# Counting the first pass of a TensorE run as longer, in the planner of a fused attention and feed-forward kernel

## The chip, the cores and the metric

The kernel runs on one core of a Trainium2 chip. The metric is the device time of one launch in microseconds, the median of a few runs of the same program. Times of single instructions come from one profiled execution, whose own time stands beside the runs below.

## The reference

The input x has 2048 rows of 640 values. It is normalised row by row, and two branches and the input itself are added up:

```python
xn = _layernorm(x, axis=-1)
return x + _A_ref(xn, A_wq, A_wk, A_wv, A_wo) + _B_ref(xn, B_w1, B_w2)

# A: 32 query heads of 20 values, one key head and one value head shared by all
q = (xn @ wq).reshape(B, S, 32, 20).transpose(0, 2, 1, 3)
k, v = xn @ wk, xn @ wv
p = softmax(einsum("bhqd,bkd->bhqk", q, k) * 20 ** -0.5)
A = einsum("bhqk,bkd->bhqd", p, v).reshape(B, S, 640) @ wo

# B: feed-forward, 640 -> 1728 -> 640
B = silu(xn @ w1) @ w2
```

The costly part is attention: 32 heads times 2048 queries times 2048 keys, that is 134 million exponentials.

## The kernel before, in words

**Tiling.** Queries are cut into 4 blocks of 512 columns, heads into 8 groups of 4, which gives 32 groups of work. Within a group the keys are cut into 16 tiles of 128. One item of work is the score tile of one head: 128 keys by 512 queries. There are 32 x 16 x 4 = 2048 items. A head has only 20 values, so its score product uses 32 of the TensorE array's 128 rows: four heads lie in four row tiles and run side by side when their instructions follow one another (line 1078, `s_mm`). In the text such a bundle is a set of scores.

**Two ways to the exponential.** Most items go to ScalarE (ACT in the profile): one ACTIVATE takes two or three score banks at once and writes exponentials (line 1166). The others go in batches of four (one key tile, four heads) to VectorE (DVE), which adds a constant to the score and writes a 16-bit integer whose bits, read as bf16, are roughly the exponential (line 1409, `p1`). Two more copies of the batch, shifted by a constant, correct that approximation; they are made by GpSimd (POOL, line 1448) or by VectorE (line 1453).

**Passes.** What is left on TensorE uses the array as four column tiles of 32 columns: the product of exponentials and values (line 1201, one pass for a key tile on ScalarE's way, three for a batch on VectorE's way, because of its shifted copies), and the projections, the feed-forward and the output product (line 447, passes of 512 columns, or of 320 for the output). A pass is four MATMULs, one for each column tile. Some output passes can be cut into row pieces that ride in a set of scores (line 454, `row_mm`). In the text a sequence of passes between two sets of scores is a run.

**Who sets the order.** The program has a fixed instruction order on each engine. A planner in Python (class `Sched`, the function `build`) makes it before the launch: it keeps a clock for each engine, gives each operation a cost in nanoseconds, and at each step commits the operation that the engine with the earliest clock would take. Engines then wait for each other on the chip by semaphores in that order. So a cost in the planner is no time on the chip; it changes only which operation is picked next. The clock of TensorE is advanced in `Sched.commit` by an operation's cost, and by `SWITCH` (97 ns to a set of scores, 98 ns to a run) when the array's use changes. `t_mc` is the cost of a pass of projections, feed-forward or output; the passes on the exponentials have a cost written at the two places that make them (`make_pv_act`, `dve_advance`). A set of n scores counts 216 + 4(n - 1) ns.

**The rule string.** The choices have thresholds (`BASE`): how far ahead of ScalarE a set of scores is issued (`need`, `hold`, `stay`), how many batches may be open at once (`open`), how long a set waits for a third bank (`patience`), whether output passes are cut into row pieces (`rows`, `half`). The string `PLAN` gives one letter to each stretch of the planner's TensorE clock, and `RULES` says which threshold the letter alters; behind the end of the string the letter is "a", which alters nothing. `PIECE` is the length of a stretch:

```python
if sc.t["pe"] >= piece * PIECE:
    ru.__dict__.update(BASE)
    ru.__dict__.update(RULES[rule(piece)])
    piece += 1
```

The letters that the prediction names: B and G cut passes of the output into row pieces (`rows` 2 or 1), f waits up to 200 ns for a third bank, J puts sets of scores off while ScalarE has more than 560 ns of work ahead, r lets VectorE's items in from 1000 ns ahead, t allows three open batches, x allows a second pass job to be begun while four banks are free, z sends every shifted copy but the third to VectorE.

Of the kernel before, what the change touches and what calls it, by code (L numbers as in the profile page):

```python
# [53 lines left out]
WAY_S = {"act": 55.0, "dve": 57.0, "pool": 57.0}  # L54
WAY_B = 57.0
SLACK_B = 1.0
WAY_DMA = -130.0
ACT_END = 104.0
DVE_END = 85.0
# [22 lines left out]
POOL_J = (2,)  # L82
SWITCH = {"s": 97.0, "p": 98.0, "f": 98.0}
SPRIO = 0.5
PIECE = 10000.0
STEPS = 1
YC = (0, 0, 3, 3)
EARLY = 1
# [17 lines left out]
RULES = dict(a={}, b=dict(keep=0.0), c=dict(lagp=3), d=dict(lagp=5), e=dict(lagp=0), f=dict(patience=200.0), g=dict(dwant=0.0),  # L106
             h=dict(zcap=4), i=dict(zcap=3), j=dict(homes=0), k=dict(leadmax=-1.0, lead=-1.0), l=dict(lead=0.08, leadmax=0.1),
             m=dict(need=740.0), n=dict(hold=0.0), o=dict(stay=640.0), p=dict(open=1), q=dict(slack=560.0), r=dict(hungry=1000.0), s=dict(claim=9), t=dict(open=3), u=dict(claim=4), v=dict(want=2), w=dict(slack=850.0), x=dict(hold2=4), y=dict(bnd=0), z=dict(pj=-1e9), A=dict(rows=0), B=dict(rows=2, rowmin=2), C=dict(pj=2000.0), D=dict(openlag=3), E=dict(pj=8000.0), F=dict(hold2=3), G=dict(rows=1), H=dict(half=0), I=dict(half=3), J=dict(stay=560.0), K=dict(stay=720.0), P=dict(need=560.0), Q=dict(hold=120.0), L=dict(uopen=3), M=dict(uopen=4), N=dict(uopen=5), O=dict(uopen=0))
PLAN = "acbgxnoQpQJvpnaQodtxzpvEoQJBJoaodpJqQaDqJovpkBrnvxBxQJBfaaooHoatano"


def rule(n):
# [55 lines left out]


def t_mc(n):  # L170
    return n / 2.4 + (9.0 if n >= 512 else 4.0)


def t_mm(n):
# [37 lines left out]
class Sched:  # L212
# [33 lines left out]
    def way(self, h, op):  # L246
        if h.eng == op.eng:
            return 0.0
        if h.dma_sem is not None:
            return WAY_DMA  # L250
        if op.eng == "pe":
# [33 lines left out]
    def commit(self, op, start):  # L285
        e = op.eng
        op.deps = self.hazards(op)
        if op.sync is not None:
            op.deps.add(op.sync)
        op.start = start  # L290
        if e == "pe":
            if op.mode != self.pe_mode:
                start += self.turn(op.mode)
                self.pe_mode = op.mode
            s0 = self.joined(op)
            if s0 is not None:
                end = max(start + op.occ, self.pe_set[2])
                self.pe_set = (s0, self.pe_set[1] | op.slots, end)
                op.fin = start + op.occ + 170.0
                op.occ = end - self.t[e]  # L300
                self.t[e] = end
            else:
                op.fin = start + op.occ + 170.0
                self.t[e] = start + op.occ
                self.pe_set = (start, op.slots, start + op.occ) if op.slots else None
        elif e == "sp":
            self.t[e] = start + op.occ
            own = 3300.0 if op.name == "dma wv" else 800.0 if op.name.startswith("dma pk") else 2000.0 if op.name.startswith("dma la") else 0.0
            self.dma_free = max(self.dma_free, start + 1300.0) + (op.lat - 800.0 if op.name.startswith("dma pk") else op.lat)
            op.fin = self.dma_free + 700.0 + own  # L310
        else:
            if op.port and e == "dve" and start > self.t[e] and start <= self.port_free["pool"] + 1.0:
                op.occ -= PORT_HID
            op.fin = start + op.occ + op.lat
            self.t[e] = start + op.occ
            if op.port:
                self.port_free[e] = start + op.occ - (PORT_GAP if e == "pool" else 0.0)
        op.done = True
        for r in op.reads:
            r.r.append(op)  # L320
        for r in op.writes:
            r.w = op
            r.r = []
        self.order[e].append(op)
        if op.on_commit is not None:
            op.on_commit(op)


def build(nc, A_x, A_wq, A_wk, A_wv, A_wo, B_x, B_w1, B_w2, out, stack):
# [90 lines left out]
    def res(*k):  # L420
        if k not in R:
            R[k] = Res()
        return R[k]
# [58 lines left out]
    def load_x(n):  # L482
# [9 lines left out]
         reads=[res("idf")], writes=[res("idf")], prio=0.02)  # L492
# [10 lines left out]
    def zeros(n, k=QW):  # L503
# [5 lines left out]
              reads=[res("zero")], writes=[res("v")], prio=0.6)  # L509
    v1s = []  # L510
    for j, cj in enumerate(C_J):
        v1s.append(pool(lambda g, j=j, cj=cj: g.memset(v_all[:, j, :, DH:DH + 1], 0.5 * cj), 120,
                        pre=[vms], writes=[res("v")], prio=0.6 + 0.01 * j))

    def wrow(ap):
# [6 lines left out]
                  reads=[res("wk")], writes=[res("wkr", r)], prio=0.08) for r in range(1, HG)]  # L522
# [4 lines left out]
    for n in range(8, NT):  # L527
# [11 lines left out]
        reads=[res("wqs0")], pre=[pool_wq0, d_wq0], writes=[res("wqp0")], prio=0.15)  # L539
# [97 lines left out]
    v_op = {}  # L637
# [568 lines left out]
    def make_pv_act(g, kt, d):  # L1206
        flags = {}

        def f(pe):
            lst = []  # L1210
            for i in range(HG):
                k = d[i][0]
                lst.append((v_all[:, 0, kt, :], Ebuf[:, k * QW:(k + 1) * QW], i))
            return pv_mms(pe, flags["bank"], lst, flags["first"], flags["last"])
        op = Op("pe", f, 224.0, pre=[x[1] for x in d.values()] + v_op[kt // 4],
                reads=[res("E", x[0]) for x in d.values()] + [res("vv", kt // 4, 0)],
                mode="p", prio=1.0, name=f"PV{g}_{kt}")
        pv_reg(op, g, flags)
        return op
# [200 lines left out]
    def dve_advance(job):  # L1420
        st = job.batch
        st["left"].remove(job.head)
        st["p1"].append(job.consumers[0])
        if st["left"]:
            return
        open_b.remove(st)
        g, kt, zi = st["g"], st["kt"], st["zi"]
        z = z_t[zi]
        zr = [res("z", zi, i) for i in range(HG)]
        N = HG * QW  # L1430
        closed.append(st)
        z16 = z[:, :].bitcast(I16)
        st["nth"] = len(closed)
        src = [([z[:, i * QW:(i + 1) * QW] for i in range(HG)], st["p1"], zr)]
        for j in range(1, NJ):
            qk = XQ[j - 1]
            if qk is not None and len(s_last[j - 1]) == NW[j - 1] and len(xq_read[qk]) == DC + FC and all(o.done for o in xq_read[qk]):
                s_last[j - 1].append(sc.order["pe"][-1])
            wi = min(range(len(s_last[j - 1])), key=lambda k: -1 if s_last[j - 1][k] is None or k == NW[j - 1] and isinstance(s_last[j - 1][k], Op) else s_last[j - 1][k]["nth"])
            old = s_last[j - 1][wi]  # L1440
            s_last[j - 1][wi] = st
            lent = wi == NW[j - 1]
            t = xnT[:, 0:HG, qk * QW:(qk + 1) * QW] if lent else s_t[j - 1][wi][:, :]
            zin = z16.rearrange("p (h q) -> p h q", h=HG) if lent else z16
            r = res("s", j, wi)
            args = dict(pre=st["p1"] + ([idb] + [norm_op[n] for n in range(NT)] if old is None else [old] if isinstance(old, Op) else [old["pv"][j]]), reads=zr, writes=[r], name=f"s{j}")
            if j in POOL_J or pool_load() < ru.pj:
                op = pool(lambda v, t=t, j=j, zin=zin: v.tensor_scalar(t.bitcast(I16), zin, float(SHIFT[j]), 1.0, ALU.add, ALU.mult),  # L1448
                          POOL_SHIFT, POOL_END, prio=0.3, **args)
                op.port = True  # L1450
                op.gate = calm(op)
            else:
                op = dve(lambda v, t=t, j=j, zin=zin: v.tensor_scalar_add(t.bitcast(I16), zin, float(SHIFT[j])), t_dve(N, 4),  # L1453
                         prio=SPRIO - 0.01 * j, **args)
                op.port = True
                op.on_commit = shifts.append
            src.append(([t[:, i, :] if lent else t[:, i * QW:(i + 1) * QW] for i in range(HG)], [op], [r]))
        st["sh"] = [pre[0] for _, pre, _ in src[1:]]
        st["pv"] = []
        for j, (t, pre, rd) in enumerate(src):  # L1460
            flags = {}

            def f(pe, t=t, j=j, flags=flags):
                lst = [(v_all[:, j, kt, :], t[i], i) for i in range(HG)]
                return pv_mms(pe, flags["bank"], lst, flags["first"], flags["last"])
            pv = Op("pe", f, 224.0, pre=pre + v_op[kt // 4], reads=rd + [res("vv", kt // 4, j)],
                    mode="p", prio=1.5, name=f"PVd{g}_{kt}")
            pv_reg(pv, g, flags)
            st["pv"].append(pv)
# [71 lines left out]
    def make_two():  # L1541
# [8 lines left out]
                   pre=[norm_op[n] for n in range(NT)] + [o for n in range(NT) for o in tr_ops[n]] if k else [])  # L1550
# [88 lines left out]
    def take(job, e):  # L1639
        b = job.fixed  # L1640
        if b is None:
            ok = [b for b in xbanks() if bank_at(b, job.ops[0].mode) <= e + SLACK_B]
            b = (min(ok, key=lambda b: (-left_over(sc.free, (b,)), HOME_ORDER.index(b))) if ru.homes else max(ok)) if ok else min(xbanks(), key=bank_free_at)
# [340 lines left out]
    while not finished():  # L1984
        if sc.t["pe"] >= piece * PIECE:
            ru.__dict__.update(BASE)
# [13 lines left out]
        es, op, what = got  # L2000
# [173 lines left out]
```

## Time and profile before

| what | value |
|---|---|
| time, median of 3 runs | 689.98 us (689.96 to 690.01) |
| the profiled execution's own time | 690.16 us |
| its span, first to last instruction | 688.3 us |
| granted TensorE clock | 1.00 |
| TensorE busy | 675.7 us (98%) |
| ScalarE busy | 666.4 us (97%) |
| VectorE busy | 591.3 us (86%) |
| GpSimd busy | 581.7 us (85%) |
| ACTIVATEs of exponentials | 656 |
| items on VectorE's way | 676, that is 169 batches |

The profile names engines PE (TensorE), PEld (its weight loads), ACT, DVE, POOL and SP (the queue of DMAs). A group's row gives the line of the kernel, the engine, the operation, the tiles written and read, their size, the count, the busy time and the mean. The row of a window gives its bounds, its length, and for each engine the busy time and the count of instructions in it. A row of the timeline gives the start and the length of a stretch of like instructions. Records of neighbouring instructions on an engine overlap, so the distance between two starts says what an instruction costs its engine, and the record's own length says more than that.

### The profile page before, as it was taken

The page shows a single profiled execution, that of the slowest core. Times are in us where ns is not written, and L with a number is a line of the kernel's source. Part 1 is how long each engine was busy: PE and PEld are TensorE (multiplying, and loading weights), DVE is VectorE, ACT ScalarE, POOL GpSimd, SP SyncE. Part 2 cuts the span into 40 slices and gives each one's busy share as a digit, 9 for nine tenths or more (in the row PEclk, how much of TensorE's full clock was granted, in tenths as well). Part 3 has the DMA queues.
Part 4 walks back from the last instruction along what each step waited for, and adds up shares of the span by engine and source line. Part 5 has one row for each costly group of instructions (what it writes and reads, how often), then busy time and mean ns, then how long its engine had stood idle before and what let it go on. Part 6 is the DMA issues. An engine that isn't in the chain of part 4 may idle for free.

```text
span 688.3 us, 22511 instructions
## 1 busy us (share of the span) xinstructions
PE 675.7 (98%) x9821; PEld 232.2 (34%) x9821; DVE 591.3 (86%) x1017; ACT 666.4 (97%) x728; POOL 581.7 (85%) x349
## 2 busy tenths in 40 slices
PE   8999999999999999999999999999999999999998
PEld 6432222222333333322323333332233333333345
DVE  7899988999989878798898897889999898987953
ACT  6999999999999999999999999999999999999992
POOL 6658899898988998899898889888889987879990
PEclk9999999999999999999999999999999999999999
DMA  8643220222221222422022222132222221223201
GB/s 226 190 160 42 19 23 14 35 34 25 23 29 12 32 38 29 72 36 30 9 22 30 29 31 33 26 37 61 31 22 20 21 27 23 32 20 70 23 7 41
DMA packets 34241, 28.97 MB, mean 42 GB/s; under 512 B 15486, under 2 KB 29662, under 8 KB 34142
## 3 DMA queue, kind: packets, MB, share of 16 engines
q1 hardware_dynamic: 33854, 27.20, 25.8%
q8 instruction: 77, 1.26, 0.8%
q10 hardware_dynamic: 288, 0.33, 0.1%
q14 instruction: 22, 0.18, 0.1%
HBM read 11.09 MB, written 2.62 MB: 20 GB/s over the span
## 4 chain that ended last, share of the span: by engine, by line
ACT 52%; PE 42%; DVE 3%; POOL 1%; DMA 0%; issue 0%; DVEq 0%; ACTq 0%
ACT sbt L1166 48%; PE psall L1201 14%; PE psall L1078 14%; PE psall L447 13%; ACT sbt L773 3%; DVE sbt L1409 2%; POOL sbt L1448 1%; PE psall L595 1%; PE psall L621 1%; DVE sbt L1453 0%; DMA sbt<-in_A_x_dram 0%; PE psall L999 0%; PE psall L1017 0%; ACT sbt L554 0%; DVE sbt L565 0%
## 5 line engine op out<-in xcount | busy, mean ns | idle before, releaser
L1166 ACT ACTIVATE sbt<-psall 128x1024 bf16<-128x1024 f32 (+1 forms) x656 | 640.0, 1138 | 3.2 <-PE psall L1078 3.0
L1448 POOL TENSOR_SCALAR sbt<-sbt 128x2048 int16<-128x2048 int16 x273 | 518.6, 1900 | 72.5 <-PE psall L1201 15.3
L1409 DVE TENSOR_SCALAR sbt<-psall 128x512 int16<-128x512 f32 x676 | 440.1, 685 | 63.1 <-PE psall L1078 58.0
L1078 PE MATMUL psall<-sbt 32*128 32x512 bf16 x2048 | 268.3, 384 | 3.3 <-ACT sbt L1166 2.0
L1201 PE MATMUL psall<-sbt 128*32 128x512 bf16 x3400 | 264.7, 384 | 1.9 <-POOL sbt L1448 0.6
L447 PE MATMUL psall<-sbt 128*32 128x320 bf16 (+2 forms) x3772 | 225.9, 332 | 2.1 <-DVE sbt L776 0.7
L1078 PEld LDWEIGHTS psall<-sbt 32*128 32x128 bf16 x2048 | 71.8, 91 | 236.9 <-ACT sbt L1166 174.1
L447 PEld LDWEIGHTS psall<-sbt 128*32 128x32 bf16 x3772 | 80.4, 95 | 85.5 <-issue 45.4
L1201 PEld LDWEIGHTS psall<-sbt 128*32 128x32 bf16 x3400 | 68.8, 94 | 115.5 <-issue 71.9
L1453 DVE TENSOR_SCALAR sbt<-sbt 128x2048 int16<-128x2048 int16 x65 | 47.6, 750 | 0.0
L860 POOL TENSOR_TENSOR sbt<-sbt 128x512 bf16<-128x512 f32 x30 | 38.3, 1277 | 4.9 <-DVE sbt L1453 2.7
L776 DVE SCALAR_TENSOR_TENSOR sbt<-sbt,psall 128x512 bf16<-128x512 bf16 x52 | 35.5, 682 | 3.8 <-ACT sbt L773 1.8
L773 ACT ACTIVATE sbt<-psall 128x512 bf16<-128x512 f32 x52 | 34.9, 671 | 0.2 <-PE psall L447 0.2
L454 PE MATMUL psall<-sbt 32*128 32x320 bf16 (+1 forms) x78 | 24.4, 313 | 0.0
L1250 DVE COPY sbt<-psall 128x512 f32<-128x512 f32 x31 | 21.2, 683 | 0.9 <-PE psall L1201 0.8
L919 DVE SCALAR_TENSOR_TENSOR sbt<-psall,sbt 128x320 f32<-128x320 f32 x8 | 3.9, 491 | 12.2 <-PE psall L447 7.0
L903 DVE SCALAR_TENSOR_TENSOR sbt<-psall,sbt 128x320 bf16<-128x320 f32 x24 | 11.6, 482 | 3.1 <-PE psall L447 1.7
L693 DVE TENSOR_SCALAR sbt<-psall 128x512 bf16<-128x512 f32 x20 | 13.5, 676 | 0.0
L572 POOL TENSOR_TENSOR sbt<-sbt 128x2 f32<-128x2 f32 x8 | 5.7, 710 | 8.5 <-DVE sbt L570 8.2
L1725 PE MATMUL psall<-sbt 128*32 128x256 bf16 (+1 forms) x188 | 11.1, 375 | 1.2 <-DVE sbt L487 1.2
L585 POOL TENSOR_SCALAR sbt<-sbt 128x640 bf16<-128x640 bf16 x12 | 10.4, 878 | 1.5 <-DVE sbt L577 1.5
L563 DVE BATCH_NORM_STATS2 sbt<-sbt 128x6 f32<-128x320 bf16 x14 | 6.6, 472 | 2.0 <-DMA sbt<-in_A_x_dram 2.0
(64 smaller groups left out, 118.3 us busy)
## 6 DMA issues: line engine op xcount, KB each, us to landing
sbt<-sbt SPq DMA_DIRECT2D x120, 64.0 KB, 3.8
sbt<-in_A_x_dram SPq DMA_DIRECT2D x28, 160.0 KB, 3.9
sbt<-sbt SPq DMA_DIRECT2D x213, 20.0 KB
out_dram<-sbt SPq DMA_DIRECT2D x14, 160.0 KB, 2.2
sbt<-in_B_w_dram SPq DMA_DIRECT2D x1, 2160.0 KB, 11.5
sbt<-in_B_w_dram SPq DMA_DIRECT2D x1, 2080.0 KB, 8.2
sbt<-sbt SPq DMA_DIRECT2D x75, 8.0 KB
sbt<-in_A_wq_dram SPq DMA_DIRECT2D x1, 800.0 KB, 6.7
```

Source lines behind the costliest of these rows:

```text
L447: ins = pe.matmul(ps[j * SLOT:(j + 1) * SLOT, b * BANK + off:b * BANK + off + n], w[:, j * SLOT:(j + 1) * SLOT], x, start=start, stop=stop ...
L454: return pe.matmul(ps[0:w.shape[-1], b * BANK:b * BANK + n], w[k], x[k], start=start, stop=stop, tile_position=(r * SLOT, 0))
L773: t = Op("act", lambda a: a.activation(t_buf[0:rows, ts, :], bk(job.bank, 0, QW, rows=rows), AF.Tanh, scale=0.5), t_act(512), ACT_END, pre ...
L776: u = Op("dve", lambda v: v.scalar_tensor_tensor(out=hT[par][0:rows, fk, :], in0=t_buf[0:rows, ts, :], scalar=1.0, in1=bk(job.bank, 0, QW, ...
L860: nm = pool(lambda e: e.tensor_tensor(oU[:, us, :], U_sb[:, us, :], Rrep, ALU.mult), 1356.0, POOL_END, pre=[uc] + lc + pack_op.get(divmod( ...
L1078: return pe.matmul(bk(b), kT_rep[i * SLOT:(i + 1) * SLOT, kt * P:(kt + 1) * P], qT[i * SLOT:(i + 1) * SLOT, g % NQ, :], start=True, stop=T ...
L1166: return a.activation(Ebuf[:, es * QW:es * QW + w], ps[:, buf[0] * BANK:buf[0] * BANK + w], AF.Exp, scale=ESCALE)
L1201: ins = pe.matmul(ps[i * SLOT:(i + 1) * SLOT, ub * BANK:ub * BANK + QW], lhsT, rhs, start=(first and k < HG), stop=(last and k >= len(lst) ...
L1250: return v.tensor_copy(U_sb[:, us, :], bk(ub))
L1409: p1 = Op("dve", lambda v: v.tensor_scalar(z16[:, i * QW:(i + 1) * QW], bk(job.bank), ZBIAS, 0.0, ALU.add, ALU.max), t_dve(QW) + 2.0, DVE_ ...
L1448: op = pool(lambda v, t=t, j=j, zin=zin: v.tensor_scalar(t.bitcast(I16), zin, float(SHIFT[j]), 1.0, ALU.add, ALU.mult), POOL_SHIFT, POOL_E ...
L1453: op = dve(lambda v, t=t, j=j, zin=zin: v.tensor_scalar_add(t.bitcast(I16), zin, float(SHIFT[j])), t_dve(N, 4), prio=SPRIO - 0.01 * j, **args)
```

## The change

Three things are altered in the planner, and no instruction of its own is added.

1. The cost of a pass on the exponentials falls from 224 to 216 ns, that of other passes by 6.3 ns (512 columns and more) or 1.3 ns (fewer). 10.4 ns are added to the first pass behind a change from another use of the array.
2. A stretch of the rule string lasts 16 us of the planner's clock instead of 10.
3. The string is another one, of 42 letters instead of 67.

```diff
+FIRST = 10.4
+PASS = 216.0
...
-PIECE = 10000.0
+PIECE = 16000.0
...
-PLAN = "acbgxnoQpQJvpnaQodtxzpvEoQJBJoaodpJqQaDqJovpkBrnvxBxQJBfaaooHoatano"
+PLAN = "apQxxcJBxtrJJfBfKcrJhoGzBKGvErjzBrPBBaaJto"
...
 def t_mc(n):
-    return n / 2.4 + (9.0 if n >= 512 else 4.0)
+    return n / 2.4 + 2.7
...
         if e == "pe":
             if op.mode != self.pe_mode:
                 start += self.turn(op.mode)
+                if op.mode == "p":
+                    op.occ += FIRST
                 self.pe_mode = op.mode
...
-        op = Op("pe", f, 224.0, pre=[x[1] for x in d.values()] + v_op[kt // 4],
+        op = Op("pe", f, PASS, pre=[x[1] for x in d.values()] + v_op[kt // 4],
...
-            pv = Op("pe", f, 224.0, pre=pre + v_op[kt // 4], reads=rd + [res("vv", kt // 4, j)],
+            pv = Op("pe", f, PASS, pre=pre + v_op[kt // 4], reads=rd + [res("vv", kt // 4, j)],
```

## The prediction

> **What bounds the kernel now.** I read the first and the fourth part of the page, then ScalarE's groups by shape, then windows of 100 us.
>
> ```profile
> span 688.3 us, 22511 instructions
> PE 675.7 (98%) x9821; PEld 232.2 (34%) x9821; DVE 591.3 (86%) x1017; ACT 666.4 (97%) x728; POOL 581.7 (85%) x349
> ACT 52%; PE 42%; DVE 3%; POOL 1%; DMA 0%; issue 0%; DVEq 0%; ACTq 0%
> ```
>
> Two engines are full, and the chain that ended last alternates between them. Busy shares don't say which one gives way, so the cost of one instruction is read from distances between starts, on ScalarE first.
>
> ```profile
> L1166 ACT ACTIVATE sbt<-psall 128x1024 bf16<-128x1024 f32 x594 | 563.5, 1100 | 2.6 <-PE psall L1078 2.5
> L1166 ACT ACTIVATE sbt<-psall 128x1536 bf16<-128x1536 f32 x61 | 89.7, 1512 | 0.6 <-PE psall L1078 0.6
> 299.68 4.76 ACT L1166 ACTIVATE sbt<-psall 128x1024 bf16<-128x1024 f32 x5
> 304.20 0.73 ACT L773 ACTIVATE sbt<-psall 128x512 bf16<-128x512 f32 x1
> 304.68 3.92 ACT L1166 ACTIVATE sbt<-psall 128x1024 bf16<-128x1024 f32 x4
> ACT sbt L1166 <- PE psall L1078: 3.0, 7, 0.6
> sum 500.00, ACT 485.06; mean ACT 97.01
> ```
>
> Five exponentials of two banks take 304.20 - 299.68 = 4.52 us, 0.904 us each, and the tanh behind them 0.48 us. The waits of ScalarE for scores come to 3.0 us in 7 places. The sum is that of five windows of 100 us from 100 to 600 us, for line 1166 alone: 97.01 of 100 us, and the tanh fills most of the rest. In steady state ScalarE has no room.
>
> TensorE comes next, as a stretch of its timeline (rows between are left out).
>
> ```profile
> 301.02 0.39 PE L1078 MATMUL psall<-sbt 32*128 32x512 bf16 x3
> 301.34 0.62 PE L447 MATMUL psall<-sbt 128*32 128x512 bf16 x8
> 301.89 0.39 PE L1078 MATMUL psall<-sbt 32*128 32x512 bf16 x3
> ...
> 304.82 0.83 PE L1201 MATMUL psall<-sbt 128*32 128x512 bf16 x12
> 305.48 0.60 PE L447 MATMUL psall<-sbt 128*32 128x512 bf16 x8
> ...
> 311.90 0.39 PE L1078 MATMUL psall<-sbt 32*128 32x512 bf16 x3
> ```
>
> A set of scores is followed 0.32 us later by a run (301.34 - 301.02). Three passes take 0.66 us (305.48 - 304.82), 0.22 each. A run of two passes reaches the next set after 0.55 us (301.89 - 301.34), which is 0.11 us more than two passes. So a set with the turn to it and back costs 0.32 + 0.11 = 0.43 us, and a pass 0.22 us.
>
> **The change part by part: the costs.** A cost moves nothing on the chip by itself; every instruction of an unchanged order would run as before. What it can do is make the planner's clock right or wrong. From 301.02 to 311.90 us there are 11 cycles of set and run, with 28 passes of 512 columns. The kernel before counts 11 x (224 + 98 + 97) + 28 x 224 = 10,881 ns; the trace has 10.88 us. The kernel after counts 11 x (224 + 98 + 97 + 10.4) + 28 x 216 = 10,771 ns, which is 0.11 us short, 10 ns for each run. The reason is in the rows: the first pass is now counted as longer, but the last one loses the 8 ns that stood for the rest of its turn. The old costs are right for a run of two to three passes and too high for long ones; the new ones are about equally short for all runs, so they rank long against short runs better, and stand worse against ScalarE's clock, whose costs are unchanged. With 656 ACTIVATEs, and about one set for each, the clock of TensorE is short by up to 656 x 10 = 6.6 us. Price on the chip: 0, where sets of scores are issued early enough that 10 ns are lost in their lead; up to +6.6 us, where each set comes late for ScalarE by that much; a gain of as much is excluded, for the order can take nothing from an instruction. I take 0, because ScalarE waited only 7 times, which is the nearest row. It holds as long as the lead holds; without that cover ScalarE waits next, for line 1078.
>
> **The change part by part: the string.** What a string can move is the number of batches that go to VectorE's way. One batch more takes four items from ScalarE, two ACTIVATEs: 2 x 0.904 = 1.81 us. On TensorE it takes two sets (0.87 us) and adds two passes (0.43 us): 0.44 us less. On VectorE it adds four instructions of line 1409, and on GpSimd one or two of line 1448:
>
> ```profile
> L1448 POOL TENSOR_SCALAR sbt<-sbt 128x2048 int16<-128x2048 int16 x273 | 518.6, 1900 | 72.5 <-PE psall L1201 15.3
> L1409 DVE TENSOR_SCALAR sbt<-psall 128x512 int16<-128x512 f32 x676 | 440.1, 685 | 63.1 <-PE psall L1078 58.0
> ```
>
> VectorE has 63.1 us and GpSimd 72.5 us idle ahead of those lines, mostly waiting for TensorE, so a few batches fit. The price of one on the path lies between 0.44 us (TensorE sets the end) and 1.81 us (ScalarE does). I take 1.81 us, since the full windows are ScalarE's. [...]
>
> How many batches the new string moves, no trace shows. The nearest rows are the stretches of the old string with the same letters, since a planner's clock of n us lies within 2 us of the trace's (the row pieces that letter B orders from 270 us show in the window 270 to 280, below). VectorE's busy time in line 1409 per 10 us of a letter, as sums of windows, in the order: the whole from 60 to 660 us, then J, x, t, B, r, f, z, then a, Q, o, v, n.
>
> ```profile
> sum 600.00, DVE 419.96; mean DVE 419.96
> sum 60.00, DVE 38.39; mean DVE 6.40
> sum 30.00, DVE 18.17; mean DVE 6.06
> sum 20.00, DVE 15.90; mean DVE 7.95
> sum 40.00, DVE 28.71; mean DVE 7.18
> sum 10.00, DVE 7.58; mean DVE 7.58
> sum 10.00, DVE 8.15; mean DVE 8.15
> sum 10.00, DVE 7.45; mean DVE 7.45
> sum 70.00, DVE 50.94; mean DVE 7.28
> sum 60.00, DVE 43.35; mean DVE 7.23
> sum 90.00, DVE 61.56; mean DVE 6.84
> sum 40.00, DVE 29.42; mean DVE 7.36
> sum 30.00, DVE 21.64; mean DVE 7.21
> ```
>
> The mean is 7.00 us in 10. Each letter's difference from it, times the tens of us by which the new string has more of it between 60 and 660 us: J -0.60 x 2.0 = -1.2; x -0.94 x 0.6 = -0.6; t +0.95 x 1.2 = +1.1; B +0.18 x 5.6 = +1.0; r +0.58 x 5.4 = +3.1; f +1.15 x 2.2 = +2.5; z +0.45 x 2.2 = +1.0; a +0.28 x -3.8 = -1.1; o -0.16 x -7.0 = +1.1; Q +0.23 x -6.0 = -1.4; v +0.36 x -2.4 = -0.9; n +0.21 x -3.0 = -0.6. The sum is +4.0 us of line 1409, which at 440.1 / 676 = 0.65 us is six items, one and a half batches more. But r, f and z, with one stretch each behind them, make +6.6 us of it; without them it is -2.6 us, four items fewer, and G, K, P, h, j and c have no such stretch at all. For the bounds I take windows of 100 us of line 1409, which hold six to ten letters each:
>
> ```profile
> 100.00:200.00 100.00, 68.40 (x107) 1.00 0.21 25
> 400.00:500.00 100.00, 71.71 (x111) 1.00 0.27 37
> sum 500.00, DVE 351.38; mean DVE 70.28
> ```
>
> The five hold 107 to 111 items. Against their middle of 109 that is 2% either way, 12 of 676 items, three batches: -5.4 to +5.4 us. I take one batch, -1.8 us, between nothing and the one and a half of the letters.
>
> **The row pieces.** Letters B and G cut passes of 320 columns into pieces that ride in sets.
>
> ```profile
> L454 PE MATMUL psall<-sbt 32*128 32x320 bf16 x70 | 21.3, 305 | 0.0
> 270.00:280.00 10.00, 2.44 (x8) 0.73 (x8) 1.00 0.11 26
> 540.00:550.00 10.00, 1.52 (x5) 0.45 (x5) 1.00 0.37 29
> 200.00:300.00 100.00, 6.70 (x22) 1.99 (x22) 1.00 0.27 37
> ```
>
> A stretch of B amid output work has 5 to 8 pieces, the 100 us around it 22, with the 8: some 4 above the usual, or one pass less in 10 us. The old string has B in output work for about 30 us, the new one B or G for about 80 us (224 to 240, 384 to 400, 416 to 432, 560 to 592): five passes less. A pass of 320 columns is 320/512 of 0.22 us, 0.14 us, so 0.7 us of TensorE, from 0 (ScalarE sets the end) to 0.7 us; by TensorE's 42% of the chain 0.3 us. Longer stretches by themselves change no instruction; I cost them at nothing, and what they may lose is in the bounds of the batches.
>
> **The sum.** 690.16 us of the profiled execution (688.3 of span and 1.9 around it) - 1.8 - 0.3 = 688.1 us. The median of the runs is 0.18 us below the profiled execution, which gives 687.9 us.
>
> **The rivals.** *Fewer batches (slower).* The letter J, with the second lowest rate above, takes 80 us of the new string. If it keeps that rate and r, f and z prove to be chance, one batch falls back to ScalarE, and by the lower bound of the windows three: 3 x 1.81 = 5.4 us, 695.4 us. It decides below 169 batches, 676 instructions of line 1409; one batch fewer already gives 691.8 us. Against it: VectorE's idle time, which leaves room for the same number. *Late sets (slower).* TensorE's clock, 10 ns short at each run, lets sets start later than planned, and ScalarE waits: up to 6.6 us, 696.6 us. It decides where ScalarE's waits for line 1078 pass the 3.0 us by more than the gain of 2.1 us. For it speaks the chain, which goes through TensorE for 42%; against it the 7 waits. The Trainium skill ("TensorEngine Tiling (Array Packing)", section "Key Properties") states that changing the tiling mode drains TensorE; the trace agrees in both directions, 0.10 us before a run and 0.11 us before a set, and the new costs leave out a part of the second. *No difference.* Gains and losses of single stretches cancel, as those of the letters nearly do: 169 batches within one either way at TensorE's price, 689.5 to 690.4 us.
>
> **How the numbers follow.** 0.2% is 1.4 us, about what a measurement of this kernel can tell from no change. More batches and passes cut: 0.43, 687.9 us, with its own range of 683.9 us (three batches and 0.7 us of passes) to 688.6 us. No difference: 0.17. Fewer batches: 0.26. Late sets: 0.14. That makes faster 0.43, same 0.17, slower 0.40. The range has to take in both sides: from 683.9 us to 696.6 us, the upper bounds of both slower rivals.
>
> **What would show it.** Right: about 680 instructions of line 1409 and some 654 of line 1166, ScalarE's waits for line 1078 near 3 us, and some 90 row pieces in line 454. Late sets would show as more and longer waits of line 1166 for 1078 at an unchanged count; fewer batches as more than 656 of line 1166, and more idle time ahead of line 1409. Wrong altogether, if the opening (first exponential at 13.64 us below) or the end behind the last one (15.44 us from 659.67, so 675.11 us) moved by more than a microsecond, for I cost both at nothing: their letters alter thresholds of the steady state.
>
> ```profile
> 13.64 1.92 ACT L1166 ACTIVATE sbt<-psall 128x1024 bf16<-128x1024 f32 x2
> 659.67 15.44 ACT L1166 ACTIVATE sbt<-psall 128x1024 bf16<-128x1024 f32 x13
> ```

## The result, and the profile after

The changed kernel takes 692.13 us, the kernel before 689.92 us beside it on the same chip: a ratio of 1.0043, with a 95% interval of 1.0032 to 1.0055. It is slower, where 687.9 us and a gain of 2 us were forecast; the time lies inside the range given, on the other side of the old one. One of the six executions of the changed kernel took 697.15 us at a mean granted clock of 0.990; it is in the ratio and lifts it above that of the medians, which is 1.0032.

The profiled execution took 692.15 us. The page of the kernel after, its first and fourth parts:

```profile
span 690.3 us, 22674 instructions
PE 676.0 (98%) x9901; PEld 234.5 (34%) x9901; DVE 589.9 (85%) x1007; ACT 668.5 (97%) x720; POOL 586.6 (85%) x352
ACT 52%; PE 41%; DVE 2%; POOL 2%; DMA 1%; SPq 1%; issue 1%; DVEq 0%; POOLq 0%
```

By its shares it is the same kernel; the difference is in counts. ScalarE's groups by shape:

```profile
L1170 ACT ACTIVATE sbt<-psall 128x1024 bf16<-128x1024 f32 x564 | 539.4, 1095 | 2.4 <-PE psall L1082 2.4
L1170 ACT ACTIVATE sbt<-psall 128x1536 bf16<-128x1536 f32 x84 | 124.6, 1508 | 0.2
```

Its waits for scores (total, count, longest, in us):

```profile
ACT sbt L1170 <- PE psall L1082: 2.4, 6, 0.5
```

The timeline of its first and its last exponentials:

```profile
14.06 1.94 ACT L1170 ACTIVATE sbt<-psall 128x1024 bf16<-128x1024 f32 x2 [0.38 <-PE psall L1082]
654.53 21.85 ACT L1170 ACTIVATE sbt<-psall 128x1024 bf16<-128x1024 f32 x20
```

And VectorE's line of items, from the groups of the page:

```profile
L1413 DVE TENSOR_SCALAR sbt<-psall 128x512 int16<-128x512 f32 x668 | 438.4, 684 | 66.6 <-PE psall L1082 60.5
```

VectorE's way took 668 items instead of 676: 167 batches, two fewer. ScalarE nevertheless has fewer exponentials, 648 instead of 656, because 23 more of them take three banks; so their count without their shapes says nothing on the batches. ScalarE's exponentials cost their engine 0.904 us with two banks and 1.331 us with three (most frequent distance between starts, the same in both traces). That makes 594 x 0.904 + 61 x 1.331 + 0.48 = 618.6 us before, and 564 x 0.904 + 84 x 1.331 = 621.7 us after. In what follows this sum is ScalarE's work. Where the 2.0 us of span come from:

| part of the span | before | after | difference |
|---|---|---|---|
| start of the first exponential | 13.64 | 14.06 | +0.4 |
| ScalarE's work | 618.6 | 621.7 | +3.0 |
| all else from the first to the end of the last exponential | 42.8 | 40.6 | -2.2 |
| behind the last exponential (675.1 and 676.4 us) | 13.2 | 13.9 | +0.7 |

Nearly all of the 2.2 us lies behind the exponentials of two banks: the distances there exceed 0.904 us by 12.5 us in all before and by 10.4 us after. The waits for scores, 3.0 and 2.4 us, are mostly a part of that; what makes up the rest I have not taken apart.

### The profile page after: what moved, and what is told of

Its sections match the earlier page's. It is cut to its first block, busy times and chain, and to the rows that moved or that the text cites. A ratio compares the mean times of both kernels' runs of the same rounds, so it can differ in the third digit from the quotient of the medians.

```text
span 690.3 us, 22674 instructions
## 1 busy us (share of the span) xinstructions
PE 676.0 (98%) x9901; PEld 234.5 (34%) x9901; DVE 589.9 (85%) x1007; ACT 668.5 (97%) x720; POOL 586.6 (85%) x352
## 4 chain that ended last, share of the span: by engine, by line
ACT 52%; PE 41%; DVE 2%; POOL 2%; DMA 1%; SPq 1%; issue 1%; DVEq 0%; POOLq 0%
ACT sbt L1170 48%; PE psall L1205 14%; PE psall L1082 13%; PE psall L451 12%; ACT sbt L777 3%; DVE sbt L1413 1%; POOL sbt L1452 1%; DMA sbt<-in_A_wq_dram 1%; DMA sbt<-sbt 1%; PE psall L625 1%; PE psall L599 0%; PE psall L1021 0%; PE psall L1003 0%; PE psall L1729 0%; SPq L860 0%
## 5 line engine op out<-in xcount | busy, mean ns | idle before, releaser
L1452 POOL TENSOR_SCALAR sbt<-sbt 128x2048 int16<-128x2048 int16 x276 | 524.3, 1900 | 70.8 <-DVE sbt L1457 24.8
L451 PE MATMUL psall<-sbt 128*32 128x320 bf16 (+3 forms) x3780 | 225.0, 332 | 1.3 <-DVE sbt L1413 0.7
L1205 PEld LDWEIGHTS psall<-sbt 128*32 128x32 bf16 x3384 | 69.0, 94 | 119.6 <-issue 73.2
L451 PEld LDWEIGHTS psall<-sbt 128*32 128x32 bf16 (+1 forms) x3780 | 82.2, 95 | 79.5 <-issue 42.0
L1457 DVE TENSOR_SCALAR sbt<-sbt 128x2048 int16<-128x2048 int16 x58 | 43.5, 764 | 0.8 <-PE psall L1205 0.7
L458 PE MATMUL psall<-sbt 32*128 32x320 bf16 (+1 forms) x90 | 28.3, 315 | 0.0
L1729 PE MATMUL psall<-sbt 128*32 128x256 bf16 (+1 forms) x264 | 16.4, 356 | 1.2 <-DVE sbt L491 1.2
L697 DVE TENSOR_SCALAR sbt<-psall 128x512 bf16<-128x512 f32 x20 | 13.5, 676 | 2.3 <-PE psall L451 2.3
L589 POOL TENSOR_SCALAR sbt<-sbt 128x640 bf16<-128x640 bf16 x12 | 10.4, 879 | 1.5 <-DVE sbt L581 1.5
L1729 PEld LDWEIGHTS psall<-sbt 128*32 128x32 bf16 x264 | 7.4, 113 | 5.9 <-issue 2.7
## 6 DMA issues: line engine op xcount, KB each, us to landing
sbt<-in_B_w_dram SPq DMA_DIRECT2D x1, 2160.0 KB, 12.5
```

The source lines that it names most:

```text
L451: ins = pe.matmul(ps[j * SLOT:(j + 1) * SLOT, b * BANK + off:b * BANK + off + n], w[:, j * SLOT:(j + 1) * SLOT], x, start=start, stop=stop ...
L458: return pe.matmul(ps[0:w.shape[-1], b * BANK:b * BANK + n], w[k], x[k], start=start, stop=stop, tile_position=(r * SLOT, 0))
L1205: ins = pe.matmul(ps[i * SLOT:(i + 1) * SLOT, ub * BANK:ub * BANK + QW], lhsT, rhs, start=(first and k < HG), stop=(last and k >= len(lst) ...
L1729: ins = pe.matmul(ps[i * SLOT:(i + 1) * SLOT, ub * BANK:ub * BANK + n], zero_t[:, 0:SLOT], zero_t[:, 0:n], start=fresh, stop=fresh, tile_p ...
```

## The experiments

Three things were changed together: costs, string, and the length of a stretch. The first four runs keep the costs alone, keep the string with its stretches alone, and take the string away altogether; a later one undoes the length of a stretch. In all of these the arithmetic is complete; only the order differs, and with it which items go to VectorE. The counts in the expectations are those of the order that the planner writes before a launch, and every trace shows them. Each time measured is of one execution, except in the last experiment.

**The costs alone.** The kernel after with the string and the stretches of before:

```diff
-PIECE = 16000.0
+PIECE = 10000.0
-PLAN = "apQxxcJBxtrJJfBfKcrJhoGzBKGvErjzBrPBBaaJto"
+PLAN = "acbgxnoQpQJvpnaQodtxzpvEoQJBJoaodpJqQaDqJovpkBrnvxBxQJBfaaooHoatano"
```

> The three new costs alone; string and stretches of 10 us as before. The order that comes out holds 620 items of VectorE's way (155 batches, 14 fewer than before) and, for ScalarE, 502 exponentials of two banks, 141 of three and one of one. Theory 'fit' (a string belongs to the costs that it was chosen with, and what it is worth is the number of batches): ScalarE's work is 502 x 0.904 + 141 x 1.331 + 0.48 = 642.0 us against 618.6 us before, so 713 us or a little more. Theory 'late sets' (the costs are short by 10 ns for each run and this is what made the change slower): 692 to 697 us, with longer waits of ScalarE for scores. Theory 'TensorE sets the end' (a batch is worth 0.44 us): 690 + 14 x 0.44 = 696 us.

Measured: 726.21 us, beside 689.57 us for the kernel before. The groups of ScalarE by shape, and its waits for scores:

```profile
L1170 ACT ACTIVATE sbt<-psall 128x1024 bf16<-128x1024 f32 x502 | 487.5, 1101 | 8.4 <-PE psall L1082 7.9
L1170 ACT ACTIVATE sbt<-psall 128x1536 bf16<-128x1536 f32 x141 | 208.6, 1556 | 10.3 <-PE psall L1082 10.3
```

```profile
ACT sbt L1170 <- PE psall L1082: 18.1, 23, 2.4
```

Fourteen batches fewer than before, and 36.6 us slower. ScalarE's work explains 23.4 of them, and 13 more are above what was expected: waits for scores are up by 15 us, and the granted clock is 0.983, of which more below. TensorE's price of 0.44 us for a batch is far off.

**The string alone,** with its stretches of 16 us; the costs are those of before:

```diff
-PIECE = 10000.0
+PIECE = 16000.0
-PLAN = "acbgxnoQpQJvpnaQodtxzpvEoQJBJoaodpJqQaDqJovpkBrnvxBxQJBfaaooHoatano"
+PLAN = "apQxxcJBxtrJJfBfKcrJhoGzBKGvErjzBrPBBaaJto"
```

> The new string and stretches of 16 us alone, with the costs of before. The order holds 636 items (159 batches, 10 fewer than before), 556 exponentials of two banks and 100 of three: 635.7 us of ScalarE's work against 618.6 us. Fit: 707 us or a little more, although neither the string nor the costs are at fault by themselves. Late sets: the costs are right again, so not slower than before by more than 1 us, 688 to 691 us. TensorE sets the end: 690 + 10 x 0.44 = 694 us.

Measured: 714.29 us, 7 us above what "fit" expected, with 14.7 us of waits for scores. The costs of before are back, and the time is not. "Late sets" expected 688 to 691 us and falls here. So neither half of the change carries its 2 us: alone they cost 36.6 and 24.7 us, together 2.2 us. The parts do not add up.

**No string,** once with each set of costs (the diff is that of the old costs; with the letter a everywhere the length of a stretch alters nothing):

```diff
-PLAN = "acbgxnoQpQJvpnaQodtxzpvEoQJBJoaodpJqQaDqJovpkBrnvxBxQJBfaaooHoatano"
+PLAN = "a"
```

> The costs of before with the letter a everywhere, that is no string. The order holds 644 items (161 batches), 561 exponentials of two banks and 94 of three: 632.3 us of ScalarE's work. Fit: 704 us, the string of before is worth 14 us. Late sets says nothing on the string. TensorE sets the end: 690 + 8 x 0.44 = 694 us.

> The new costs with the letter a everywhere. The order holds 612 items (153 batches), 491 exponentials of two banks, 151 of three and one of one: 645.3 us of ScalarE's work, 13 us more than with the costs of before and no string. Fit: 717 us, so that the new string is worth 25 us, and had to regain what the new costs lost. Late sets: at most 7 us above the run with old costs and no string. TensorE sets the end: 690 + 16 x 0.44 = 697 us.

Measured: 704.56 us with the old costs and 724.94 us with the new ones; the second is 8 us above what was expected. ScalarE's groups with the old costs and no string:

```profile
L1166 ACT ACTIVATE sbt<-psall 128x1024 bf16<-128x1024 f32 x561 | 540.8, 1129 | 2.7 <-PE psall L1078 2.6
L1166 ACT ACTIVATE sbt<-psall 128x1536 bf16<-128x1536 f32 x94 | 142.7, 1555 | 3.2 <-PE psall L1078 3.2
```

Each string is worth much with its own costs: 15 us for the old, 33 us for the new one. With the letter a everywhere the old costs give the better order; with the new string the new costs do, by 22 us (692.13 against 714.29). The sign goes with the string.

This can mean that a string fits its costs because truer or less true costs call for other thresholds, or that any nudge deals a new hand. The next runs separate the two.

**0.4 ns less for the first pass.**

```diff
-FIRST = 10.4
+FIRST = 10.0
```

> The changed kernel with 10.0 ns instead of 10.4 ns for the first pass of a run: 0.4 ns in the planner, nothing on the chip. The order is the same up to about 118 us and holds 648 items of VectorE's way (162 batches against 167), 545 exponentials of two banks, 103 of three and one of one: 630.2 us of ScalarE's work against 621.7 us. Theory 'draw' (which order comes out of a string and costs is close to a draw; the string is chosen for one such draw): 700.6 us or more, that is over 8 us for 0.4 ns. Theory 'costs' (truer costs give a better order, a little truer or less true a little better or worse): 692 us within 1 us.

Measured: 703.16 us, 11 us more for 0.4 ns in the planner. ScalarE's groups:

```profile
L1170 ACT ACTIVATE sbt<-psall 128x1024 bf16<-128x1024 f32 x545 | 520.7, 1099 | 2.2 <-PE psall L1082 2.0
L1170 ACT ACTIVATE sbt<-psall 128x1536 bf16<-128x1536 f32 x103 | 151.3, 1510 | 2.2 <-PE psall L1082 1.9
```

The order holds five batches fewer, and 8.5 of the 11 us are ScalarE's work (630.2 against 621.7 us). The theory "costs", by which a small step in a cost makes a small step in the time, falls.

**The turn as the trace has it.**

```diff
-SWITCH = {"s": 97.0, "p": 98.0, "f": 98.0}
+SWITCH = {"s": 106.0, "p": 98.0, "f": 98.0}
```

> The changed kernel with 106 instead of 97 ns for the turn from a run to a set of scores, as the trace has it. This takes away the 10 ns by which the new costs fall short for each run. The order holds 636 items (159 batches), 538 exponentials of two banks and 112 of three: 635.4 us of ScalarE's work. Draw: 706 us or more, although the costs are truer. Late sets: at or below 692 us, with shorter waits of ScalarE for scores. Costs: below 692 us.

Measured: 712.76 us. In the stretch that the prediction reads, these costs count 11 x (224 + 98 + 106 + 10.4) + 28 x 216 = 10,870 ns against 10.88 us in the trace. They are nearer to it than those of the kernel after, and the order is 21 us slower. ScalarE's waits for scores:

```profile
ACT sbt L1170 <- PE psall L1082: 8.9, 14, 3.6
```

"Late sets" expected shorter waits than the 2.4 us of the kernel after, and they are longer.

**One letter.**

```diff
-PLAN = "apQxxcJBxtrJJfBfKcrJhoGzBKGvErjzBrPBBaaJto"
+PLAN = "apQxxcJBxtrJJaBfKcrJhoGzBKGvErjzBrPBBaaJto"
```

> The changed kernel with the letter a in place of the first f (from 208 to 224 us); nothing else. The order is the same up to about 219 us, and holds 648 items in all (162 batches), 565 exponentials of two banks and 90 of three: 630.5 us of ScalarE's work. Theory 'letter' (a letter acts in its own stretch, where f costs VectorE items): at or below 692 us, with more than the 16 items of line 1413 from 208 to 224 us. Draw: no worse in that stretch, but 701 us or more in all, because every later stretch is dealt anew.

Measured: 704.15 us. Windows of VectorE's items in the kernel after, first the stretch of the letter, then a late one:

```profile
208.00:224.00 16.00, 9.87 (x16) 1.00 0.08 13
500.00:600.00 100.00, 71.47 (x111) 1.00 0.21 23
```

and in the kernel with the other letter:

```profile
208.00:224.00 16.00, 11.40 (x18) 1.00 0.11 13
500.00:600.00 100.00, 64.70 (x99) 1.00 0.19 21
```

In its own stretch f does cost two items, 16 against 18, as theory "letter" has it. But 300 us later, where the two strings have the same letters, the order now passes 99 items instead of 111. What this letter does where it stands is small beside what it does to everything behind it. "Draw" stands for the total, "letter" for the stretch alone.

**The stretches alone.** The kernel after, with stretches of 10 us:

```diff
-PIECE = 16000.0
+PIECE = 10000.0
```

> The changed kernel with its new string in stretches of 10 us instead of 16: the third part of the change undone alone. The order holds 632 items (158 batches), 522 exponentials of two banks and 124 of three: 636.9 us of ScalarE's work against 621.7 us. Draw: 708 us or more, for the string was fit to stretches of 16 us too. If the length of a stretch did nothing by itself, as the prediction costed it, 692 us.

Measured: 722.92 us, against 708 us or more expected, so the length of a stretch can't be costed by itself either.

**Another string for the old costs.** Thirteen letters differ and three are added behind the end, sixteen in all where the expectation says seventeen:

```diff
-PLAN = "acbgxnoQpQJvpnaQodtxzpvEoQJBJoaodpJqQaDqJovpkBrnvxBxQJBfaaooHoatano"
+PLAN = "acbgxnoQpQuvpnDQodtxzpvEoQJGoomodpPqQoDqJovpkBrnvFBxQJBfmcooHoPKpnooza"
```

> The kernel before with 17 of its letters changed or added behind the end, its costs and its stretches of 10 us kept. The string was looked for with those costs among some thousand neighbours of the old one, by what the planner's order holds. It has 676 items of VectorE's way, as before, 593 exponentials of two banks and 62 of three: 618.6 us of ScalarE's work, the same as before. Draw, with ScalarE's work setting the time: within 1 us of before, 689 to 690.5 us, although the order differs from 100 us on. Theory 'letter' (letters act by their rates): m, P, F, K and c for J, a, o and Q would move more than 1 us.

Measured: 688.96 us against 689.59 us, a ratio of 0.999 with an interval of 0.9981 to 0.9999. It is the fastest of the kernels here, by a margin just clear of nothing, and a shade under the 689 us that were expected at least. ScalarE's work is the same 618.6 us, and the time is within 1 us, although the order differs from 100 us on. The string had been chosen for the counts that its order holds, so this shows what equal work makes of the time, and not what a string chosen blindly would do.

**All runs side by side.** ScalarE's work from the counts of each trace (two banks 0.904 us, three 1.331 us); waits are those of ScalarE for scores; the last column is the time between the first and the last exponential in which TensorE's granted clock was half.

| kernel | batches | two / three banks | ScalarE's work | span | span less work | waits | clock at half |
|---|---|---|---|---|---|---|---|
| other_draw | 169 | 593 / 62 | 618.6 | 687.1 | 68.5 | 3.9 | 0 |
| before | 169 | 594 / 61 | 618.6 | 688.3 | 69.7 | 3.0 | 0 |
| after | 167 | 564 / 84 | 621.7 | 690.3 | 68.6 | 2.4 | 0 |
| first_10_0 | 162 | 545 / 103 | 630.2 | 701.3 | 71.1 | 3.9 | 6.8 |
| one_letter | 162 | 565 / 90 | 630.5 | 702.4 | 71.9 | 9.1 | 3.4 |
| no_string_old_costs | 161 | 561 / 94 | 632.3 | 702.8 | 70.5 | 5.8 | 0 |
| turn_106 | 159 | 538 / 112 | 635.4 | 711.0 | 75.6 | 8.9 | 6.8 |
| string_only | 159 | 556 / 100 | 635.7 | 712.5 | 76.8 | 14.7 | 3.4 |
| stretch_10 | 158 | 522 / 124 | 636.9 | 721.1 | 84.2 | 17.7 | 23.9 |
| costs_only | 155 | 502 / 141 | 642.0 | 724.4 | 82.4 | 18.1 | 23.9 |
| no_string_new_costs | 153 | 491 / 151 | 645.3 | 723.1 | 77.8 | 13.5 | 17.1 |

Over the four kernels whose clock never fell, span less work stays within 68.5 to 70.5 us, while the work goes from 618.6 to 632.3 us. That is the shown part: ScalarE's work sets the time of these kernels, to within 2 us. In the others the remainder grows with the waits and, where it is largest, with the time at half clock.

## Why the prediction was wrong, point by point

**What bounds the kernel: right.** ScalarE is full, and the kernels differ by its work. The price of a batch was put at 1.81 us. Between before and after two batches cost 3.0 us of work, 1.5 each, because 23 more exponentials of three banks save a little; from before to no_string_old_costs eight batches cost 13.7 us, 1.71 each. TensorE's price of 0.44 us a batch is refuted by every run with seven or more batches fewer than before: seven would cost 3.1 us by it, and first_10_0 lost 13.2 us.

**The number of batches: the step that failed.** It was taken as one more, from each letter's rate in the old string, with the remark that the sign hangs on r, f and z. It was two fewer: in place of the term of -1.8 us stand +3.0 us of ScalarE's work. VectorE's busy time in its line of items in the kernel after, as sums of windows of 16 us between 60 and 660 us, in the order J, x, t, B, r, f, z, K:

```profile
sum 80.00, DVE 56.18; mean DVE 11.24
sum 32.00, DVE 21.81; mean DVE 10.91
sum 32.00, DVE 21.96; mean DVE 10.98
sum 96.00, DVE 69.73; mean DVE 11.62
sum 64.00, DVE 48.59; mean DVE 12.15
sum 32.00, DVE 19.01; mean DVE 9.50
sum 32.00, DVE 21.98; mean DVE 10.99
sum 32.00, DVE 19.92; mean DVE 9.96
```

Divided by 1.6 for 10 us: J 7.02 (6.40 in the old string), x 6.82 (6.06), t 6.86 (7.95), B 7.26 (7.18), r 7.59 (7.58), f 5.94 (8.15), z 6.87 (7.45), and K, which had no stretch before, 6.23. Only r and B kept their rates. f, which was to bring 2.5 us of items, lost 3.4 us against the mean of 7.00, K 2.5 us; at 0.65 us an item that is nine items, about the eight that went. But one_letter forbids reading this as the cause: with the f taken out the total got worse. A rate seen in a stretch of 10 us belongs to that stretch of that order, not to the letter. The error was to carry it over. The bound has the same fault: windows of 100 us of one chosen string scatter by three batches, while the orders here whose string was not chosen for exactly their costs and stretches hold seven to sixteen batches fewer than before. That two fewer lies within three is luck as far as the argument goes, for nothing in those windows tells how well a new string is fit to new costs.

The working was not complete either. The sum leaves out seven letters that the old string has in these 600 us (p, d, q, k, D, E and H), and for n it takes a stretch that begins at 50 us instead of the one at 650 us. With these put right it comes to about +6 us, nine items more, which is still farther from what happened. And the sign named for fewer batches, more than 656 of line 1166, did not show: there are 648, for the reason given with the result.

**The costs at 0: right in its mechanism, wrong as a part of a sum.** Sets of scores did not come late (2.4 us of waits against 3.0 us), although the planner's clock of TensorE is short by 10 ns for each run. But the costs were priced as if they did nothing else. With the old string they take away 14 batches, and with none eight. The three parts of the change were priced one by one and added; the runs show that they can't be.

**The longer stretches at nothing: wrong in the same way.** Undone alone they cost 31 us (722.92 against 692.13).

**The row pieces: fewer than forecast.** Some 90 were forecast, counted from 70 of 320 columns and 20 more. The kernel before also has 8 of 512 columns (first line); the two others are the groups of the line after:

```profile
L454 PE MATMUL psall<-sbt 32*128 32x512 bf16 x8 | 3.1, 385 | 0.0
L458 PE MATMUL psall<-sbt 32*128 32x320 bf16 x78 | 23.7, 304 | 0.0
L458 PE MATMUL psall<-sbt 32*128 32x512 bf16 x12 | 4.6, 384 | 0.0
```

So there are twelve more, 90 against 78: three passes' worth and not five. What they are worth, forecast as 0.3 us, no run here isolates.

**The rivals.** "Fewer batches" is what happened, near its own price: 690.16 + 2 x 1.81 - 0.3 = 693.5 us for the profiled execution, which took 692.15. "Late sets" did not happen. The opening and what follows the last exponential, costed at nothing, moved by 0.4 and 0.7 us.

## What to carry to other kernels

Where a planner with many thresholds writes the order, a change to its costs is a new draw of the whole order. Price it by what the order that comes out deals to the full engine, counted in instructions and by their shapes, and do not add up its parts or carry rates from one order to another. The order is written before the launch, so these counts can be had without the chip. A tuned string of thresholds belongs to one set of costs: before new costs are kept, they need a string of their own at least as good, and here that string was two batches short.

## What the runs showed of the hardware

I had not expected TensorE's clock to fall in a kernel that never lets it rest for long. In costs_only it did so five times. Windows of that trace, with the busy time of PE, PEld, DVE, ACT and POOL, then the granted clock (the last two numbers are the DMA share and GB/s):

```profile
536.50:539.90 3.40, 2.00 (x22) 0.54 (x14) 3.29 (x6) 3.40 (x5) 3.24 (x3) 0.99 0.15 11
539.90:543.30 3.40, 3.38 (x29) 0.81 (x27) 2.15 (x5) 2.40 (x3) 3.24 (x3) 0.50 0.03 7
543.30:546.70 3.40, 1.88 (x24) 0.58 (x21) 3.06 (x5) 3.40 (x3) 3.32 (x2) 1.00 0.08 20
546.70:553.50 6.80, 6.45 (x76) 2.16 (x72) 2.77 (x5) 5.62 (x5) 5.95 (x4) 0.50 0.02 4
```

In these rows a stretch of 3.4 us in which TensorE was busy for 1.9 or 2.0 us is followed by 3.4 or 6.8 us at half clock, in which ScalarE runs dry (2.40 of 3.40 us). The Trainium skill ("TensorE: Matmul & The Clock Gate", section "Why this matters for your kernels") asks for no idle gaps over about 3 us between bursts. The trace differs: in the first of these stretches TensorE stood idle for 1.4 us in all (3.40 - 2.00), in the third for 1.5 us, and the clock fell all the same. The trace's clock records add that the five falls begin at 362.37, 396.50, 539.86, 546.68 and 570.58 us. These lie 10, 42, 2 and 7 times 3.413 us apart, so in this trace the clock fell only at steps of that length. The kernel after comes near such a fall. Its f from 208 us is shared with first_10_0, where the clock falls; the first row is of the kernel after, in which it does not:

```profile
209.00:212.40 3.40, 2.52 (x30) 0.68 (x20) 3.14 (x6) 3.40 (x4) 3.24 (x3) 1.00 0.00 0
```

```profile
208.80:212.20 3.40, 2.35 (x26) 0.67 (x18) 3.14 (x7) 3.40 (x5) 3.23 (x3) 0.99 0.00 0
212.20:215.60 3.40, 3.36 (x26) 0.75 (x30) 1.79 (x3) 2.73 (x4) 3.24 (x3) 0.50 0.11 29
```

What exactly decides between the two stays open. In costs_only itself a stretch with TensorE busy for 2.05 of 3.40 us, hardly more than in the first row above, kept its clock:

```profile
157.60:161.00 3.40, 2.05 (x28) 0.55 (x28) 1.71 (x3) 3.40 (x5) 1.02 (x1) 1.00 0.04 7
161.00:164.40 3.40, 2.89 (x44) 0.95 (x40) 2.26 (x5) 3.40 (x4) 2.77 (x2) 1.00 0.07 13
```

Whether the clock falls in some executions of the kernel after, one of which was granted 0.990, is not shown: only one left a trace, and its clock stayed at 1.00.

Whether the new costs would give better orders with a string searched for as long as the old one also stays open; the runs show only that this string, with these costs, is two batches short of the old pair.
